# Third column group of the first ffn layer by seven products, with one buffer for turned weights and queries loaded by halves

## The chip, the cores and the metric

The kernel runs on one core of a Trainium2 chip. The metric is the device time of one launch in microseconds (us). All arithmetic is in fp32. TensorE is called PE below, its weight loads PEld, VectorE DVE, ScalarE ACT, GpSimd POOL, SyncE SP; "SPq" is SP's queue, which issues almost all DMAs.

## The reference, cut to what matters

```python
scores = scale * np.matmul(q, k.transpose(0, 1, 3, 2))        # q, k, v: (8, 8, 576, 64)
thresh = np.max(scores, axis=-1, keepdims=True) - tau
scores = np.where(scores >= thresh, scores, -1000000000.0)
attn = np.exp(scores - np.max(scores, axis=-1, keepdims=True))
attn = attn / (np.sum(attn, axis=-1, keepdims=True) + 1e-09)
x = np.matmul(attn, v)      # then (B,H,S,D) -> (4608 tokens, 512)
...
a = x @ w_a                 # w_a, w_b: (512, 1536)
b = x @ w_b
return (a * b @ w_out)      # w_out: (1536, 512)
```

The weights arrive as float64 and are turned into fp32 on the chip.

## The kernel before, in words

**Attention.** A pair is two heads of one batch; there are 32 pairs. A unit (i, u) is a tile of 128 queries of pair i (u = 0 to 3), or its last 64 queries (u = 4). The main loop (lines 760 to 842) has one step g for each unit, and an order written out by hand: `scores` (line 314: PE fills two PSUM tiles, DVE reduces the maximum), `turn_back`, `exchange_blocks`, `turn_blocks` of the unit before (DVE transposes in 32x32 blocks, then SP writes them to a `swap` tile in DRAM, lines 437 and 449), a portion of the ffn, `weigh` (ACT exp, DVE threshold and sum), `prep` of a coming pair, a second portion of the ffn, `weighted` of the unit four steps back (PE: product with v, line 475), `normalise`, loads, stores, two more portions of the ffn. `turn_back` (line 454) reads a finished `swap` tile back into a tile `wT`, the turned weights that `weighted` needs; `wT` has WT_BUFS = 2 buffers. The tile framework gives a buffer to a new tile when the old one's last reader is done. Every engine's queue keeps the order of the program.

**Queries and keys.** `load` (line 134) brings q and k of one pair by four DMAs each on SP's queue (576 x 64 per head, in pieces of 32 floats), q four steps and k three steps ahead; `prep` (line 294) turns a whole tile in place by one DVE transpose (line 297). `qT` and `kT` have HP = 4 buffers each. For the first four pairs PE does the turning (`prep_pe`, `turn_pe`, `diagonals`).

**Blocks for the ffn.** 256 tokens make a block; there are 18: two halves of each of 8 batches, and two blocks of the batches' last 64 tokens ("tail"). A block's x is a tile of 128 partitions x 4 x 256, written head pair by head pair. When it is complete, `exchange_blocks` (line 487) has POOL write a copy `xS` whose two halves of 64 partitions are swapped (eight copies, line 485), and the block joins the list `blocks`. `xT`, `xS`, the tail tile and early raw weights share six buffers (XT_BUFS).

**The ffn of a block** (`ffn`, line 549) is a generator that yields after each small group of matmuls; `advance` runs it for as many moving columns as the step's pace allows. PE is used as four tiles of 64x64: four matmuls, two row halves times two column halves, run side by side; I call them a quad. First layer: w_a and w_b have three column groups of 512 columns; a step f covers 256 of them, so f = 0..5, and f = 4, 5 are the third group. For each f and each matrix there are 8 quads of 256 columns (line 574) into one PSUM tile `pab`; ACT copies w_a's result to `h` (line 580), DVE multiplies w_b's result in (line 582). PSUM has four such tiles ("banks", two banks each), shared by scores (two), `pab`, `pv`, `po`. Second layer (line 617): already by seven products over 2x2 halves instead of eight, from the second block on (`state["sums"]`; the first block takes the long form, line 661), with sums of `h` made by POOL (`h_sums`, line 594) and sums of the outputs (line 586) by POOL, or by DVE once the attention is over (`state["over"]`). `h` has six buffers of 2 x 256.

**Pace.** A step may run 0.09 of a block's columns, in four portions (0.3, 0.35, 0.15, 0.2), but not more than what spreads the backlog to the next block's arrival, plus a part for a backlog of over one block. Blocks left over run after the last unit, with nothing else on the chip.

Of the kernel before, what the change touches and what calls it, by code (L numbers as in the profile page):

```python
# [24 lines left out]
XT_BUFS = 6  # L25
WT_BUFS = 2
H_BUFS = 6
OSB_BUFS = 5
# [23 lines left out]
def kernel(  # L52
# [81 lines left out]
    def load(i, name, engine=nc.sync):  # L134

        b, hp = pairs[i]
        src = {"q": q, "k": k}[name]
        t = work.tile([P, NB, Q], FP32, tag=name + "T", bufs=HP, name=name + "T")
        for j in range(2):
            rows = src[b, 2 * hp + j].rearrange("(n e) d -> e n d", e=Q)  # L140
            for h in range(2):
                r = slice((2 * j + h) * Q, (2 * j + h + 1) * Q)
                engine.dma_start(t[r], rows[:, :, h * Q:(h + 1) * Q])  # L143
        loaded.setdefault(i, {})[name] = t
# [40 lines left out]
    state = {"loaded": 0, "added": 0, "converted": 0, "rows": 0, "sums": False, "through": 0, "over": False}  # L185
# [5 lines left out]
    sums_of = sums_sb.rearrange("p (f n w) -> p f n w", n=3, w=CH)  # L191

# [101 lines left out]
    def prep(i, name):  # L294

        mT = loaded[i][name].rearrange("p n e -> p (n e)")
        nc.vector.transpose(mT, mT)
        prepared.setdefault(i, {})[name] = mT

    def prep_pe(i, name):  # L300

        m = loaded[i][name]
        mT = work.tile([P, S], FP32, tag=name + "T", bufs=HP, name=name + "T")
        tp = banks(SH, "tp")
        for c in range(2):
            for n in range(NR // 2):
                nc.tensor.transpose(tp[:, c, n * R:(n + 1) * R], m[:, c * (NR // 2) + n], ident[0:R, 0:R])
        prepared.setdefault(i, {})[name] = mT
        return mT, tp
# [4 lines left out]
    def scores(i, u):  # L314
        qT, kT = prepared[i]["q"], prepared[i]["k"]
        n = 2 if u < NT else 1
        sc = [banks(SH, "sc") for _ in range(n)]
        each = [(c, t, j) for c in range(2) for t in range(n) for j in range(2)]
        if units.index((i, u)) < BY_HEAD:
            each.sort(key=lambda x: x[2])  # L320
        for c, t, j in each:
            r = slice(j * D, (j + 1) * D)
            o = t if u < NT else 1 - j
            q0, to = (u * P + t * D if u < NT else MAIN), slice(o * D, (o + 1) * D)
            nc.tensor.matmul(sc[j if u < NT else 0][to, c], qT[r, q0:q0 + D],  # L325
                             kT[r, c * SH:(c + 1) * SH], start=True, stop=True)
        mx = small.tile([P, 2], FP32, tag="mx", name="mx")
        thr = small.tile([P, 2], FP32, tag="thr", name="thr")
        bias = small.tile([P, 2], FP32, tag="bias", name="bias")
        for j in range(n):  # L330
            c = slice(j, j + 1)
            nc.vector.tensor_reduce(mx[:, c], sc[j], axis=AX.XY, op=ALU.max)  # L332
        nc.vector.tensor_scalar(thr[:, 0:n], mx[:, 0:n], cut, None, op0=ALU.subtract)
        scored[i, u] = (sc, thr, bias, mx)
# [49 lines left out]
    def diagonals(i, u):  # L384

        ws, rcp = weights[i, u]
        dg = work.tile([P, 2, P], FP32, tag="h", bufs=H_BUFS, name="dg")
        for j in range(2):
            nc.scalar.activation(dg[:, j], ident, AF.Copy, scale=rcp[:, j:j + 1])
        weights[i, u] = (ws, dg)  # L390

    def turn_pe(i, u):
# [3 lines left out]
        wT = work.tile([P, NSLOT, P], FP32, tag="wT", bufs=WT_BUFS, name="wT")  # L396
# [57 lines left out]
    def turn_back():  # L454

        while ready:
            i, h = ready.pop(0)
            n = width(i, h)
            wT = work.tile([P, NSLOT, n], FP32, tag="wT", bufs=WT_BUFS, name="wT")
# [26 lines left out]

    def exchange_blocks():
        while complete:
# [4 lines left out]
            blocks.append(((x, xs), what))  # L493
# [54 lines left out]

    def ffn(xT, what):
# [3 lines left out]
        x, xs = xT  # L553
        hs = []
        n = CH // P
# [3 lines left out]
        for f, c0, c1 in steps:  # L559
            while (state["converted"] < 2 * HP * (f // n + 1)  # L560
# [3 lines left out]
            if c0 == 0:  # L564
                hs.append(work.tile([P, 2, HALF], FP32, tag="h", bufs=H_BUFS, name="h"))
            ht = hs[f][:, :, c0:c1]
            for w in (wa_sb, wb_sb):
# [15 lines left out]
                yield c1 - c0, 0, 0  # L583
        if state["sums"]:
# [21 lines left out]
            for both in ((1, 4), (2, 5), (7, 6), (3,)):  # L606
                po = banks(len(both) * CH, "po").rearrange("p r (m w) -> p r m w", w=CH)
                left = whole = len(both) * NF // 2 * CH
                for y, m in enumerate(both):
                    k, u, other = seven[m]  # L610
                    for f in range(NF // 2):
# [12 lines left out]
                        if m == 2 and f == NF // 2 - 1:  # L624
                            h_sums((1, 0), (1, 0), (0, 0), ALU.subtract)
                        if left:
# [62 lines left out]
    def cost():  # L689

        return BLOCK_COLS - (NF // 2 * CH if state["sums"] else 0)
# [3 lines left out]
    def advance(cols):  # L695
        running["owed"] += cols
        while running["owed"] > 0:
            if running["ffn"] is None:
                if not blocks:
                    running["owed"] = 0.0  # L700
                    return
                running["ffn"] = ffn(*blocks.pop(0))
# [23 lines left out]
    def backlog():  # L726
        return len(blocks) * cost() + (running["left"] if running["ffn"] is not None else 0)
# [14 lines left out]
    first = {i: g for g, (i, u) in enumerate(units) if u == 0}  # L742

# [16 lines left out]
    for g in range(len(units) + PV_LAG):  # L760
# [7 lines left out]
        turn_back()  # L768
# [27 lines left out]
        for p in range(HP, NPR):  # L796
            for name, d in (("q", 2), ("k", 1)):
                if g == first[p] - d:
                    prep(p, name)
        if g > BY_PE:  # L800
            advance(PORTIONS[1] * pace)
            n = g - PV_LAG
            if BY_PE <= n < len(units) and part(*units[n]):
                make_room()
                weighted(*part(*units[n]))
                running["owed"] -= (NSLOT + 1) // 2 * width(*part(*units[n]))
        for n in early.get(g, [])[:1]:
# [15 lines left out]
        for p in range(HP, NPR):  # L823
            for name, d in (("q", 4), ("k", 3)):
                if g == first[p] - d:
# [18 lines left out]
    exchange_blocks()  # L844
    state["over"] = True
    while blocks or running["ffn"] is not None:
# [35 lines left out]
```

## Time and profile before

| | |
|---|---|
| times of six runs | 1472.71, 1468.56, 1470.64, 1469.78, 1469.73, 1474.5 us; median 1470.21 us |
| the profiled execution | 1472.71 us, of which 1470.9 us are the span that the profile covers, 1.8 us lie around it |
| TensorE clock granted over the span | 0.995 |
| busy: PEld, DVE, ACT, POOL | 1213.2, 941.6, 677.5, 334.3 us |
| DMA | 220.75 MB, 150 GB/s on the mean; queue q1 (SP) has 216.52 MB of it |

The profile's page sums busy time by engine, cuts the span into 40 slices of 36.8 us, follows back the chain of work that ended last, and groups instructions by line and shape. An fp32 matmul stands in the trace as two matmul records and two weight loads. Records of one quad overlap, so a record's mean length is longer than its share of the time; rates are read from the distance between starts, or from busy time in a window.

### The profile page before, as it was taken

What the parts mean: (1) busy time and instruction counts of PE and PEld (TensorE: products, weight loads), DVE (VectorE), ACT (ScalarE), POOL (GpSimd) and SP (SyncE); (2) the same over time, 40 slices, a digit from 0 to 9 for tenths busy, and PEclk for the clock granted to TensorE, in tenths of its full rate; (3) what the DMA queues carried; (4) which work ended last, traced back from release to release, by engine and by line L of the source; (5) the groups of instructions that cost most, each with busy time, mean ns of one, the idle gap of its engine ahead of it and who ended that gap; (6) DMA issues with size and microseconds to landing.
All of it is one profiled execution on the core that took longest, in us unless ns stands there. A gap on an engine that the chain in (4) does not pass through costs nothing.

```text
span 1470.9 us, 57132 instructions
## 1 busy us (share of the span) xinstructions
PE 1418.8 (96%) x25344; PEld 1213.2 (82%) x25344; DVE 941.6 (64%) x2097; ACT 677.5 (46%) x1243; POOL 334.3 (23%) x504
## 2 busy tenths in 40 slices
PE   5779999999999999999999999999999999999998
PEld 4667677888879898897888998889888888888886
DVE  6998677677666776776656765577656766613212
ACT  5886455555554554554434544354544544411010
POOL 2773503122030403031312212120404040410000
PEclk9999999999999999999999999999999999999999
DMA  9967898798858976795647876588757976530000
GB/s 192 223 187 181 178 177 192 175 178 181 199 142 167 183 192 148 159 189 145 147 97 150 182 168 149 117 191 182 162 126 145 197 178 151 132 90 16 2 17 16
DMA packets 624582, 220.75 MB, mean 150 GB/s; under 512 B 542928, under 2 KB 612048, under 8 KB 624336
## 3 DMA queue, kind: packets, MB, share of 16 engines
q1 hardware_dynamic: 621968, 216.52, 67.4%
q8 instruction: 199, 3.26, 0.9%
q10 hardware_dynamic: 2368, 0.59, 0.2%
q14 instruction: 47, 0.39, 0.1%
HBM read 127.40 MB, written 89.65 MB: 148 GB/s over the span
## 4 chain that ended last, share of the span: by engine, by line
PE 86%; DVE 6%; DMA 4%; ACT 2%; SPq 2%; issue 1%; DVEq 0%; ACTq 0%
PE pab L574 46%; PE po L617 19%; PE sc L325 10%; PE pv L475 9%; DMA swap<-tw 2%; PE po L661 1%; DVE mx L332 1%; DVE tw L363 1%; DVE tw L429 1%; SPq L437 1%; DMA kT<-in_k_dram 1%; SPq L143 1%; DMA sums_u<-in_moe_w_a_dram 1%; DMA sums_u<-in_moe_w_b_dram 1%; DVE low L238 1%
## 5 line engine op out<-in xcount | busy, mean ns | idle before, releaser
L332 DVE TENSOR_REDUCE mx<-sc 128x1 f32<-128x576 f32 x288 | 205.2, 749 | 115.1 <-PE sc L325 104.3
L574 PE MATMUL pab<-xS,wa_sb 64*64 64x256 f32 (+1 forms) x3584 | 271.2, 370 | 1.3 <-issue 1.3
L574 PE MATMUL pab<-xS,wb_sb 64*64 64x256 f32 (+1 forms) x3584 | 267.8, 370 | 0.0
L325 PE MATMUL sc<-kT,qT 64*64 64x288 f32 x2304 | 244.1, 410 | 21.0 <-DVE kT L312 9.1
L574 PE MATMUL pab<-xT,wa_sb 64*64 64x256 f32 (+1 forms) x3200 | 237.8, 369 | 6.7 <-DVE tw L363 3.2
L586 POOL TENSOR_TENSOR h<-h 128x256 f32<-128x256 f32 x168 | 117.4, 732 | 547.5 <-PE po L617 544.4
L617 PE MATMUL po<-wo_sb,h 64*64 64x256 f32 x3264 | 241.4, 376 | 0.0
L574 PE MATMUL pab<-xT,wb_sb 64*64 64x256 f32 (+1 forms) x3200 | 236.2, 368 | 4.1 <-DVE h L582 2.7
L382 ACT ACTIVATE tw<-tw,rcp 128x576 f32<-128x576 f32 x244 | 176.1, 768 | 132.7 <-DVE rcp L376 132.6
L360 ACT ACTIVATE tw<-sc,bias,scalars 128x576 f32<-128x576 f32 x260 | 216.0, 831 | 19.3 <-DMA swap<-tw 10.4
L363 DVE SCALAR_TENSOR_TENSOR tw<-sc,thr,tw 128x576 f32<-128x576 f32 x260 | 203.7, 802 | 22.6 <-ACT tw L360 21.9
L574 PEld LDWEIGHTS pab<-xS,wa_sb 64*64 64x64 f32 x3584 | 194.5, 133 | 28.7 <-POOL xS L485 2.1
L574 PEld LDWEIGHTS pab<-xS,wb_sb 64*64 64x64 f32 x3584 | 195.3, 133 | 22.7 <-issue 0.2
L617 PEld LDWEIGHTS po<-wo_sb,h 64*64 64x64 f32 x3264 | 178.9, 132 | 22.9
L574 PEld LDWEIGHTS pab<-xT,wa_sb 64*64 64x64 f32 x3200 | 172.0, 133 | 30.4 <-DVE kept L465 4.3
L574 PEld LDWEIGHTS pab<-xT,wb_sb 64*64 64x64 f32 x3200 | 171.5, 133 | 24.7 <-DVE h L582 2.9
L325 PEld LDWEIGHTS sc<-kT,qT 64*64 64x64 f32 x2304 | 146.0, 134 | 52.6 <-issue 16.1
L475 PE MATMUL pv<-wT,vm 64*64 64x320 f32 (+3 forms) x2592 | 186.7, 377 | 1.7 <-DVE h L582 1.7
L617 PE MATMUL po<-sums_u,h 64*64 64x256 f32 x2448 | 181.3, 376 | 0.0
L429 DVE STREAM_TRANSPOSE tw<-tw 128x576 f32<-128x576 f32 x240 | 171.6, 753 | 0.0
L582 DVE TENSOR_TENSOR h<-h,pab 128x512 f32<-128x512 f32 (+1 forms) x112 | 73.4, 656 | 145.6 <-PE pab L574 139.5
L475 PEld LDWEIGHTS pv<-wT,vm 64*64 64x64 f32 x2592 | 143.7, 133 | 20.5 <-DVE h L582 2.6
(83 smaller groups left out, 1242.4 us busy)
## 6 DMA issues: line engine op xcount, KB each, us to landing
swap<-tw SPq DMA_DIRECT2D x240, 288.0 KB, 5.3
wT<-swap SPq DMA_DIRECT2D x28, 1440.0 KB, 7.5
wT<-swap SPq DMA_DIRECT2D x32, 1152.0 KB, 6.3
vm<-in_v_dram SPq DMA_DIRECT2D x32, 288.0 KB, 4.9
qT<-in_q_dram SPq DMA_DIRECT2D x112, 72.0 KB, 3.5
kT<-in_k_dram SPq DMA_DIRECT2D x112, 72.0 KB, 5.1
swap<-wt SPq DMA_DIRECT2D x112, 72.0 KB, 2.7
out_dram<-kept SPq DMA_DIRECT2D x30, 256.0 KB, 4.3
```

Source lines behind the costliest of these rows:

```text
L143: engine.dma_start(t[r], rows[:, :, h * Q:(h + 1) * Q])
L325: nc.tensor.matmul(sc[j if u < NT else 0][to, c], qT[r, q0:q0 + D], kT[r, c * SH:(c + 1) * SH], start=True, stop=True)
L332: nc.vector.tensor_reduce(mx[:, c], sc[j], axis=AX.XY, op=ALU.max)
L360: nc.scalar.activation(wb[j], sb[j], AF.Exp, bias=bias[:, j:j + 1], scale=e_scale)
L363: nc.vector.scalar_tensor_tensor(out=wv, in0=sb[j], scalar=thr[:, j:j + 1], in1=wv, op0=ALU.is_ge, op1=ALU.mult, accum_out=sums[:, j:j + 1])
L382: nc.scalar.activation(w, w, AF.Copy, scale=rcp[:, j:j + 1])
L429: nc.vector.transpose(w, w)
L475: nc.tensor.matmul(pv[j * D:(j + 1) * D, r], vm[rows, k0], wT[rows, k0], start=(s == (NT if j == r else 0)), stop=(s == NT - 1))
L574: nc.tensor.matmul(pab[c * D:(c + 1) * D, r], w[rows, f // n, k, fs + c * D:fs + (c + 1) * D], moving, start=(k == 0), stop=(k == H - 1))
L582: nc.vector.tensor_tensor(ht, ht, pab, op=ALU.mult)
L586: (nc.vector if state["over"] else nc.gpsimd).tensor_tensor(*a, **kw)
L617: nc.tensor.matmul(po[c * D:(c + 1) * D, r, y], ht[rows, t0:t0 + D], other[rows, f], start=(f == 0), stop=(f == NF // 2 - 1))
```

## The change

The third column group of the first layer is computed by seven products over 2x2 halves instead of eight. The three halvings are: the two matrices w_a and w_b; the 512 input features (two times 256); the block's 256 tokens (two times 128). Products have 128 moving columns. They need sums of weights, made once (`first_sums`), and sums of x, made by POOL for each block (`x_sums`, four operations on x and four on xS), and sums of products (ACT, DVE and POOL in `seven_of`). Storage is laid out anew: `wT` becomes one constant area (`turned_sb`), and `turn_back` is moved behind `weighted` in the step; q is loaded in two halves (256 and 320 queries) with three smaller buffers; `qT` and `dg` of the first four pairs live in the area that the weight sums take later; `h` has three buffers of twice the size. A block waits in `complete` until the block before it has left its first layer; only then are `xS` and the sums made.

```diff
-XT_BUFS = 6
-WT_BUFS = 2
-H_BUFS = 6
+XT_BUFS = 7
+H_BUFS = 3
+Q_BUFS = 3
...
     def load(i, name, engine=nc.sync):
...
+        n0, n1 = {"k": (0, NB), "q0": (0, HALF // Q), "q1": (HALF // Q, NB)}[name]
+        bufs = HP if name == "k" else Q_BUFS
...
-                engine.dma_start(t[r], rows[:, :, h * Q:(h + 1) * Q])
+                engine.dma_start(t[r], rows[:, n0:n1, h * Q:(h + 1) * Q])
...
-    def turn_back():
-
-        while ready:
+    def turn_back(count):
+
+        for _ in range(count):
             i, h = ready.pop(0)
             n = width(i, h)
-            wT = work.tile([P, NSLOT, n], FP32, tag="wT", bufs=WT_BUFS, name="wT")
+            wT = turned_at((i - 1) % HP * NSLOT * TAIL if n < HALF and i else NSLOT * HALF if n < HALF else 0, n)
             nc.sync.dma_start(wT, swaps.pop((i, h)).rearrange("(s r) p w -> (r p) s w", r=G))
...
+    def x_sums(x):
+
+        t = x_tile("xU").rearrange("p m (k n) -> p m k n", k=2)
+        b11, b12, b21, b22 = (x[:, k * 2:k * 2 + 2, n * P:(n + 1) * P] for k in range(2) for n in range(2))
+        for m, a, b in ((0, b12, b11), (1, b22, t[:, 0]), (2, b22, b12), (3, t[:, 1], b21)):
+            nc.gpsimd.tensor_tensor(t[:, m], a, b, op=ALU.subtract)
+        return t
+
     def exchange_blocks():
-        while complete:
+        while complete and not state["layer"] and not blocks:
             x, what = complete.pop(0)
             xs = x_tile("xS")
             for hp in range(HP):
                 exchange(x, xs, hp, 0, HALF, nc.gpsimd)
-            blocks.append(((x, xs), what))
+            blocks.append(((x, xs) + ((x_sums(x), x_sums(xs)) if state["first"] >= 3 else ()), what))
...
+    def first_sums(n):
...
+        nc.gpsimd.tensor_tensor(out, a, b, op=op)
+        state["first"] = n + 1
+
+    def seven_of(x, hg):
...
+        for m in (1, 6, 7, 5, 2, 4, 3):
+            w, moving = products[m]
+            pab = banks(2 * P, "pab")
+            left = 2 * HP * P
+            for y in range(2):
+                for k in range(HP):
+                    for r in range(2):
+                        rows = slice(r * D, (r + 1) * D)
+                        for c in range(2):
+                            w0 = y * P + c * D
+                            nc.tensor.matmul(pab[c * D:(c + 1) * D, r, y * P:(y + 1) * P], w[k][rows, w0:w0 + D],
+                                             moving[k][rows], start=(k == 0), stop=(k == HP - 1))
+                    left -= P
+                    if left:
+                        yield P, left, 2 * HP * P
+            got = pab.rearrange("p r (f n) -> p r f n", f=2)
+            if m in (1, 7, 5):
+                nc.scalar.copy(keep({1: "t1", 7: "t7", 5: "t5"}[m]), pab)
+            if m == 6:
+                nc.vector.tensor_tensor(keep("u2"), kept["t1"], pab, op=ALU.add)
+            elif m == 7:
+                pool(kept["t7"], kept["u2"], kept["t7"], op=ALU.add)
+            elif m == 5:
+                pool(kept["u2"], kept["u2"], kept["t5"], op=ALU.add)
+                pool(kept["t5"], kept["t7"], kept["t5"], op=ALU.add)
+            elif m == 2:
+                nc.vector.tensor_tensor(kept["t1"], kept["t1"], pab, op=ALU.add)
+            elif m == 4:
+                nc.vector.tensor_tensor(kept["t7"], kept["t7"], pab, op=ALU.subtract)
+                nc.vector.tensor_tensor(h0, *(kept[z].rearrange("p r (f n) -> p r f n", f=2) for z in ("t1", "t7")),
+                                        op=ALU.mult)
+            elif m == 3:
+                nc.vector.tensor_tensor(kept["u2"], kept["u2"], pab, op=ALU.add)
+                nc.vector.tensor_tensor(h1, *(kept[z].rearrange("p r (f n) -> p r f n", f=2) for z in ("u2", "t5")),
+                                        op=ALU.mult)
+            yield P, 0, 0
...
+            if f == (NG - 1) * n and len(xT) == 4:
+                groups.append(work.tile([P, n, 2, HALF], FP32, tag="h", bufs=H_BUFS, name="h"))
+                hs += [groups[-1][:, y] for y in range(n)]
+                yield from seven_of(xT, groups[-1])
+                break
...
                         if m == 2 and f == NF // 2 - 1:
                             h_sums((1, 0), (1, 0), (0, 0), ALU.subtract)
+                            state["layer"] = False
+                            exchange_blocks()
...
-        return BLOCK_COLS - (NF // 2 * CH if state["sums"] else 0)
+        return BLOCK_COLS - (NF // 2 * CH if state["sums"] else 0) - (2 * HP * P if state["first"] >= 3 else 0)
...
+                if len(blocks[0][0]) == 4 and state["first"] == 3:
+                    first_sums(3)
...
-        turn_back()
+        back = len(ready)
         exchange_blocks()
...
-            for name, d in (("q", 2), ("k", 1)):
-                if g == first[p] - d:
+            for name, d in (("q0", 2), ("k", 1), ("q1", 1)):
+                if g == (second if name == "q1" else first)[p] - d:
                     prep(p, name)
...
                 weighted(*part(*units[n]))
                 running["owed"] -= (NSLOT + 1) // 2 * width(*part(*units[n]))
+            turn_back(back)
...
-            for name, d in (("q", 4), ("k", 3)):
-                if g == first[p] - d:
+            for name, d in (("q0", 4), ("k", 3), ("q1", 3)):
+                if g == (second if name == "q1" else first)[p] - d:
                     load(p, name)
...
+        if g > first[HP] + 1 and not converting and state["first"] < 3:
+            first_sums(state["first"])
```

Here `second[p]` is the step of pair p's unit u = 2, and `state["layer"]` is set when a block's first layer begins.

## The prediction

> **What bounds the kernel now.** I read the page's busy times and slices first, then the busy time by stretches, then the chain that ended last.
>
> ```profile
> PE 1418.8 (96%) x25344; PEld 1213.2 (82%) x25344; DVE 941.6 (64%) x2097; ACT 677.5 (46%) x1243; POOL 334.3 (23%) x504
> ...
> PE   5779999999999999999999999999999999999998
> PEld 4667677888879898897888998889888888888886
> DVE  6998677677666776776656765577656766613212
> ```
>
> PE is full from the fourth slice to the last; no other engine comes near. The busy time by stretches (time, PE, PEld, DVE, ACT, POOL, granted clock, DMA share, GB/s) shows where it is not quite full:
>
> ```profile
> 240.00:400.00 160.00, 156.85 (x2704) 136.74 (x2700) 116.75 (x265) 84.08 (x152) 33.59 (x58) 0.99 0.85 187
> 400.00:520.00 120.00, 118.11 (x2077) 102.37 (x2073) 85.46 (x193) 60.50 (x111) 31.64 (x50) 1.00 0.80 170
> 520.00:720.00 200.00, 198.75 (x3563) 175.03 (x3559) 131.08 (x297) 94.97 (x170) 35.57 (x60) 1.00 0.73 160
> 1310.00:1380.00 70.00, 70.00 (x1297) 57.95 (x1289) 14.94 (x32) 6.82 (x13) 3.96 (x10) 1.00 0.03 10
> ```
>
> From 520 us on PE idles under 1% of the time, up to 520 us some 2%. Attention ends near 1320 us; then PE works through nearly three leftover blocks alone. The chain from 1300 us on, in order of time, gives the price of one layer:
>
> ```profile
> 1327.80 17.49 PE po L617 x325
> 1345.93 40.80 PE pab L574 x757
> 1387.37 17.49 PE po L617 x325
> 1405.50 40.80 PE pab L574 x757
> ```
>
> A first layer runs from 1345.93 to 1387.37, 41.44 us for 6 column steps x 2 matrices, so 41.44 / 12 = 3.453 us for one result of 8 quads x 256 = 2048 columns: 1.686 ns a column. What PE no longer has to do comes off the end almost whole, wherever it lay, as long as PE stays full.
>
> **The matmuls.** A third column group is 2 steps x 2 matrices = 4 results: 4 x 3.453 = 13.81 us. It becomes 7 products of 2 x 4 quads of 128 columns. Does a quad of 128 cost half of one of 256, with a weight load for half the columns? The first block ran in this shape. In the busy time of line 574 alone (time, PE, PEld):
>
> ```profile
> 54.61:55.48 0.87, 0.87 (x41) 0.87 (x36) 1.00 1.04 228
> ```
>
> This is one result half: 4 quads of 128, 512 columns, in 0.87 us (1.70 ns a column). Others of these runs that nothing interrupts take 0.87 too. So a product is 2 x 0.873 = 1.746 us and seven are 12.22 us: 13.81 - 12.22 = **1.59 us a block saved**. The weight loads just fit in: they were busy for all of that window, where they take 82% of PE's time in 256-column work. Bounds: 1.71 us (no loss by the narrower shape: 13.81 / 8) and, by the interrupted runs of 0.92 us, 13.81 - 7 x 1.84 = 0.93 us.
>
> [...] The window above has a load in every 27 ns, four tiles of the array loading side by side, and the measurement decides.
>
> How many blocks? The sums of weights wait for the conversion of the weights, which ends near step 15, and are made in steps 22 to 24. The block of steps 20 to 31 is exchanged before that, as is the first; the other **16 of 18** get the sums. 16 x 1.59 = **25.5 us less**.
>
> **Evacuation of PSUM (an added wait).** The group had 2 ACT copies and 2 DVE multiplications; it gets 3 copies (580 ns) and 6 DVE operations of 512 elements (674 ns, line 582): 0.6 us on ACT and 2.7 us on DVE a block, where PE spends some 75 us. As busy time that is covered: DVE has a third of its time free. But a PSUM tile now fills in 1.75 us instead of 3.45. During about half of a step the scores hold two of the four tiles; if then an evacuation ends more than 1.75 us after its product, PE stands still, and behind the waiting matmul are the next scores.
>
> ```profile
> ACT h L580 <- PE pab L574: 173.1, 61, 6.6
> DVE h L582 <- PE pab L574: 139.5, 41, 6.3
> ```
>
> ACT stood ready in 61 of 112 cases, DVE in only 41. I measured in the timeline, for each of the 112 pairs, from the end of the result's last matmul to the end of its evacuation. After 1310 us: 0.62 us ACT, 0.79 us DVE. From 520 to 1310 us the mean excess over 1.74 us is 0.15 us (ACT) and 0.25 us (DVE); from 300 to 520 us 0.40 and 0.71 us. With 3 ACT and 4 DVE evacuations: 3 x 0.15 + 4 x 0.25 = 1.45 us for a block in the middle (11 blocks), 3 x 0.40 + 4 x 0.71 = 4.04 us early (the two blocks between 262 and 410 us), nothing for the last three. All of it: 11 x 1.45 + 2 x 4.04 = 24 us. I take a quarter, since the scores hold their tiles for half the step and the pace lets only some two products through meanwhile: **+6 us**, with ends 0 and 24.
>
> [...]
>
> **POOL.** Per block 8 sums of 256 elements (732 ns, line 586) and 3 of 512 (about 1.3 us, between 732 ns and the 1.84 us of 768 elements): 9.8 us, 157 us in all; POOL goes from 23% to about a third. The row for swapped copies is 0.396 us x 8 = 3.2 us; they now start only when product 2 of the second layer is through, behind at most 12 x 0.73 us of `h` sums that began 2.6 us earlier: 9.4 us. PE has four more products to do, 4 x 2.59 = 10.4 us, and then 1.73 us that read only `xT`. Just covered; without cover up to 3 us a block. The x sums need 5.9 us and are used 28 us later. They delay output sums and so stores on SP by some us; nothing waits for those. DVE's durations beside a busy POOL are what they are without (the maximum: 747 and 748 ns), so more POOL work is no price on DVE. I take 0.
>
> **One buffer for turned weights.** `turn_back` now waits on SP for the products of the same step, behind it are loads for three steps ahead and one store.
>
> ```profile
> L460 SPq DMA_DIRECT2D wT<-swap x64: 376/382/1732, 110.7 to 1300.2; - x64
> ...
> DMA to landing us min/median/max: 3.5/6.7/8.9
> ```
>
> In the half with one result every two steps: two steps last 14.6 us early (the shortest neighbours 11.7), 16.4 later; less 2.2 us for the products and 0.4 for the issue, 12.0 us remain (shortest 9.1) for a landing of 6.7, at most 8.9. Covered, so 0. Were it short by a us, each of 28 such reads would cost PE that us, 28 us.
>
> **Queries by halves.** 28 x 4 more DMA issues on SP; an issue has a median of 0.6 us (line 143): 67 us over 1130 us, on a queue that also waits a lot. What suffers are key loads (DVE waits for them 6.1 us in all) and swap writes while DMA is at 85%, before 410 us. The other way, reads no longer stand at a step's head waiting for the swap to land (93.2 + 31.5 us of SP's waits). The chain has 1.7% swap landing, 0.8% and 0.6% SP issue, 0.7% key landing: 56 us is the most that could go or double. Nearest row 6.1 us: I take **+2 us**, ends -5 and +15. [...] `h` by double buffers costs 0: what frees a buffer precedes the next block's matmuls on PE.
>
> **Sum.** 1472.7 - 25.5 + 6 + 2 = 1455.2 us against the profiled execution (span 1470.9 + 1.8 around it). The median of the runs is 2.5 us below that execution: **1453 us**, -1.2%.
>
> **Rivals.**
> 1. *Evacuation becomes the bound (slower).* Place: third column group, PSUM tiles of lines 580 and 582 inside the attention. If DVE is everywhere as late as from 300 to 520 us (6 operations in a row instead of 2 push it there) and each excess counts: 13 x 4.04 = 52 us; -25.5 + 52 = +27: 1497 us. It decides from 25.5 / 13 = 2.0 us a block. For it: DVE late in 71 of 112 cases. Against: the median lateness of 0.82 us after 520 us, and waits of PE for DVE there of about 1 us in all.
> 2. *Little arrives.* If the steps of the attention are paced by their own DVE, ACT and DMA chain, only the last three blocks give: 3 x 1.59 = 4.8 us, 1465 us. For it: swap landings on the chain up to 365 us. Against: PE at 99% after 520 us.
> 3. *One buffer is late (slower).* +28 us by the above with the saving of 17.5: 1481 us. Against: 2 to 5 us of slack.
> 4. *Not what it says:* the sums ready later, say four blocks without: 1459 us.
> 5. *Clean.* No price at all: 1445 us; with -5 us from SP, 1440.
>
> **Numbers.** Forecast (1444 to 1461) 0.62; clean or better, below 1444, 0.04; rival 2 (1461 to 1473) 0.14; rival 4 0.04; rival 1 0.11; rival 3 0.05. The range of 1442 to 1470 leaves out rivals 1 and 3, a little of rival 2 and of the clean end. 0.2% is 2.9 us, about what a measurement can tell from no change: faster (below 1467.3) takes the forecast, clean, rival 4 and 0.10 of rival 2: 0.80; same 0.04; slower 0.16.
>
> **What would show it.** Matmuls of 64x128 in line `seven_of` at 0.87 us for 32 records; 224 x 2 x 16 = 7168 of them; the last two blocks' first layers 39.8 us instead of 41.4. Wrong if PE idles more than 10 us longer in the attention: before `pab` with DVE or ACT as releaser (rival 1), before `pv` with a DMA (rival 3), before scores with `kT` (queries); or if 32 narrow records take over 0.98 us, where the saving is gone.

## The result, and the profile after

The changed kernel takes 1476.7 us (median of 19 runs), the kernel before 1470.84 us beside it (43 runs): ratio **1.0041**, 95% interval 1.0032 to 1.0051. It is slower by 0.4% where 1.2% less was forecast. The profiled execution took 1479.74 us, its span is 1477.8 us, the granted clock over it 0.993. One of the twelve runs of a kernel below (side edits alone) was a slow one, 1496.39 us; without it that kernel's median is 1466.3 us instead of 1466.9.

A part of the difference goes with the clock. Its mean over the runs is 0.9943 in after and 0.9951 to 0.9960 in the four batches of before; among the runs of before, a clock lower by 0.001 goes with some 1.1 us more. That would be 1 to 2 of the 5.9 us. Whether the clock is a cause here or follows from the work, no run tells.

The page of the changed kernel, busy times and PE's slices:

```profile
PE 1409.1 (95%) x28416; PEld 1225.9 (83%) x28416; DVE 1000.3 (68%) x2195; ACT 685.9 (46%) x1259; POOL 489.2 (33%) x678
...
PE   5879999989999999999999999999999999999998
```

PE looks as full as before. It has 3072 matmul records more, which is 16 blocks x 192 (a block's third group had 4 x 64 = 256 records and has 7 x 64 = 448): the change reached the 16 blocks that were counted on. Its busy time fell by 1418.8 - 1409.1 = 9.7 us, not by 25.5, so the work that is left got 15.8 us longer. And PE now idles 1477.8 - 1409.1 = 68.7 us, before 1470.9 - 1418.8 = 52.1: 16.6 us more. Together 32.4 us are missing, and they are the 25.5 us of the forecast plus the 6.9 us by which the span grew.

The busy time by stretches of the changed kernel (columns as in the prediction):

```profile
240.00:400.00 160.00, 153.44 (x3004) 136.96 (x3000) 120.89 (x272) 83.61 (x151) 48.46 (x69) 0.98 0.83 182
400.00:520.00 120.00, 116.55 (x2304) 93.73 (x2298) 89.20 (x197) 58.22 (x107) 48.19 (x73) 1.00 0.74 155
520.00:720.00 200.00, 197.17 (x4150) 168.04 (x4146) 141.38 (x314) 98.08 (x177) 55.76 (x79) 1.00 0.75 168
1310.00:1380.00 70.00, 70.00 (x1505) 67.57 (x1501) 21.39 (x38) 8.01 (x16) 20.79 (x31) 1.00 0.14 38
```

Each stretch of the attention has more idle time of PE than before (6.6 us against 3.2, 3.5 against 1.9, 2.8 against 1.3); the stretch after it has none. The chain after 1340 us shows the same from its other side:

```profile
1356.00 27.36 PE pab L683 x507
...
1383.58 11.95 PE pab L622 x437
...
1395.63 18.13 PE po L728 x333
...
1413.98 27.36 PE pab L683 x506
```

Here all is as forecast. From one first layer to the next are 57.98 us, before 59.57: 1.59 us less, predicted 1.59. Seven products run from 1383.58 to 1395.63, 12.05 us, predicted 12.22. So the loss lies in the attention: the last unit's scores begin at 1284.0 us in the trace of before and at 1299.2 in that of after, 15.2 us later, though PE has less to do until then; after that mark the changed kernel is 8.3 us shorter.

What PE waits for between 240 and 1310 us in the changed kernel (engine, tile and line, what ended the wait: us in all, times, longest; before, no row is over 2.1 us in all):

```profile
PE pab L622 <- issue: 12.2, 11, 2.2
PE po L728 <- DVE t L640: 5.1, 4, 1.6
PE sc L337 <- issue: 4.1, 2, 3.4
PE pab L622 <- DVE u L631: 1.9, 2, 1.6
PE pab L622 <- DVE tw L375: 1.9, 2, 1.0
```

Line 622 is the matmul of the seven products, line 728 that of the second layer. Rows 2, 4 and 5 are waits for DVE; rows 4 and 5 stand where rival 1 put them, before `pab`, row 2 stands before the second layer's tile `po`. The largest row isn't for DVE: "issue" means that PE waited for nothing that the profile shows, no buffer and no semaphore, eleven times, each in the middle of a product. The timeline of one case (start, us, engine, line, operation, [idle before <- releaser]):

```profile
1181.49 1.52 PE L622 MATMUL pab<-xU,wb_sb 64*64 64x128 f32 x42
...
1185.23 0.77 PE L622 MATMUL pab<-xU,wb_sb 64*64 64x128 f32 x19 [2.21 <-issue]
```

After 42 of a product's 64 records PE stands still for over 2 us, with the tile, the weights and the x that it already uses.

**Theories.** (a) *Instructions* ("fetch theory" below): PE's instructions come by DMA, and come too late. The page lists their queue (packets, MB, share of 16 engines), before and after:

```profile
q8 instruction: 199, 3.26, 0.9%
```

```profile
q8 instruction: 223, 3.65, 1.0%
```

That is 16.4 KB a packet; PE began 57247 instructions (records, loads, semaphores) in after, 256 for each packet. A narrow product is 128 of them in 1.746 us, 73 a us; 256-column work is half that, 37 a us. So narrow work eats a packet in 3.5 us instead of 7. (b) *Evacuation* (reading results out of PSUM): seven results are read in place of four, and DVE, ACT and POOL are late (rival 1). (c) *The side edits* (queries by halves, one `wT`, order of the loads) cost something.

### The profile page after: what moved, and what is told of

It reads as the page before. It is cut to its first block, busy times and chain, and to the rows that moved or that the text cites. A ratio compares the mean times of both kernels' runs of the same rounds, so it can differ in the third digit from the quotient of the medians.

```text
span 1477.8 us, 63772 instructions
## 1 busy us (share of the span) xinstructions
PE 1409.1 (95%) x28416; PEld 1225.9 (83%) x28416; DVE 1000.3 (68%) x2195; ACT 685.9 (46%) x1259; POOL 489.2 (33%) x678
## 4 chain that ended last, share of the span: by engine, by line
PE 84%; DVE 7%; ACT 3%; issue 3%; DMA 2%; SPq 1%; ACTq 0%; DVEq 0%
PE pab L683 33%; PE po L728 20%; PE pab L622 11%; PE pv L491 10%; PE sc L337 9%; DVE mx L344 2%; PE po L774 1%; DVE tw L445 1%; DVE tw L375 1%; DMA swap<-tw 1%; SPq L154 1%; ACT tw L372 1%; DMA sums_u<-in_moe_w_b_dram 0%; DMA sums_u<-in_k_dram 0%; DVE xT L481 0%
## 5 line engine op out<-in xcount | busy, mean ns | idle before, releaser
L375 DVE SCALAR_TENSOR_TENSOR tw<-sc,thr,tw 128x576 f32<-128x576 f32 x260 | 202.5, 802 | 15.2 <-ACT tw L372 14.5
L588 POOL TENSOR_TENSOR t<-u,t 128x512 f32<-128x512 f32 x14 | 17.8, 1273 | 533.2 <-ACT t L629 533.2
L683 PE MATMUL pab<-xS,wa_sb 64*64 64x256 f32 (+1 forms) x2560 | 186.5, 368 | 0.4 <-issue 0.4
L683 PE MATMUL pab<-xS,wb_sb 64*64 64x256 f32 (+1 forms) x2560 | 182.9, 367 | 0.0
L491 PE MATMUL pv<-turned_sb,vm 64*64 64x320 f32 (+3 forms) x2592 | 179.0, 378 | 2.8 <-DVE h L691 1.7
L683 PE MATMUL pab<-xT,wb_sb 64*64 64x256 f32 (+1 forms) x2304 | 164.4, 367 | 4.5 <-DVE h L691 2.7
L683 PE MATMUL pab<-xT,wa_sb 64*64 64x256 f32 (+1 forms) x2304 | 158.5, 366 | 4.6 <-DVE tw L375 3.2
L491 PEld LDWEIGHTS pv<-turned_sb,vm 64*64 64x64 f32 x2592 | 133.0, 132 | 28.3 <-issue 3.5
L683 PEld LDWEIGHTS pab<-xS,wa_sb 64*64 64x64 f32 x2560 | 139.2, 134 | 15.5 <-POOL xS L501 2.1
L683 PEld LDWEIGHTS pab<-xS,wb_sb 64*64 64x64 f32 x2560 | 137.9, 133 | 13.3 <-issue 0.3
L728 PEld LDWEIGHTS po<-sums_u,h 64*64 64x64 f32 x2448 | 125.9, 134 | 20.6
L683 PEld LDWEIGHTS pab<-xT,wb_sb 64*64 64x64 f32 x2304 | 121.6, 134 | 18.8 <-DVE h L691 2.9
```

The costliest lines, as they stand in the source:

```text
L375: nc.vector.scalar_tensor_tensor(out=wv, in0=sb[j], scalar=thr[:, j:j + 1], in1=wv, op0=ALU.is_ge, op1=ALU.mult, accum_out=sums[:, j:j + 1])
L491: nc.tensor.matmul(pv[j * D:(j + 1) * D, r], vm[rows, k0], wT[rows, k0], start=(s == (NT if j == r else 0)), stop=(s == NT - 1))
L588: (nc.vector if state["over"] else nc.gpsimd).tensor_tensor(*a, **kw)
L683: nc.tensor.matmul(pab[c * D:(c + 1) * D, r], w[rows, f // n, k, fs + c * D:fs + (c + 1) * D], moving, start=(k == 0), stop=(k == H - 1))
L728: nc.tensor.matmul(po[c * D:(c + 1) * D, r, y], ht[rows, t0:t0 + D], other[rows, f], start=(f == 0), stop=(f == NF // 2 - 1))
```

## The experiments

### The parts alone

**Side edits alone.** The changed kernel without the sums of weights, so without products:

```diff
-        if g > first[HP] + 1 and not converting and state["first"] < 3:
-            first_sums(state["first"])
```

> The changed kernel without the seven products: the sums of the weights are never made, so all blocks take the long form of the third column group; one buffer for turned weights, its later read, queries by halves, double h buffers and the delayed exchange stay. Fetch theory (PE's instruction stream runs dry in the narrow products while the DMA engines are loaded) and evacuation theory (PE waits for PSUM tiles of the narrow products) both expect the time of the kernel before, 1467 to 1475 us. Side theory (the single buffer, the SP queue or the delayed exchange cost the 30 us that are missing) expects 1490 to 1505 us.

Measured: 1466.9 us, ratio 0.9971 (0.9959 to 0.9982). The side edits do not cost, they gain some 4 us. PE's idle time from 240 to 520 us falls from 5.0 us to 2.65:

```profile
240.00:520.00 280.00, 277.35 (x4854) 244.97 (x4850) 204.55 (x471) 146.43 (x264) 66.03 (x108) 1.00 0.84 180
```

Theory (c) falls, and the products are to be measured against 1466.9: with 25.5 us saved it would be 1441.4, and 35.3 us are to be found.

**Narrow matmuls alone.** The kernel before, whose third group runs in halves of 128 columns: the same four results, the same evacuations, only twice as many instructions for them.

```diff
-                for k in range(H):
+                for t0, k in [(z, k) for z in (range(0, c1 - c0, P) if f // n == NG - 1 else (0,)) for k in range(H)]:
+                    t1 = t0 + P if f // n == NG - 1 else c1 - c0
...
-                            nc.tensor.matmul(pab[c * D:(c + 1) * D, r],
+                            nc.tensor.matmul(pab[c * D:(c + 1) * D, r, t0:t1],
```

> The kernel before, its third column group computed as before, but each result in two halves of 128 columns: twice the instructions for it, the same columns, the same four evacuations at the same distance of 3.5 us. PE's own time grows by 16 x 0.873 - 13.81 = 0.16 us a block, 3 us in all. Fetch theory: 1 to 2 us more for each of some 15 blocks inside the attention, 1489 to 1504 us, with PE waits of the kind issue in the middle of the narrow runs. Evacuation theory: 1472 to 1476 us.

Measured: 1501.1 us, ratio 1.0202 (1.0172 to 1.0233). Its largest wait from 240 to 1310 us:

```profile
PE pab L575 <- issue: 12.8, 11, 2.2
```

Eleven waits for nothing, as in after, with no new evacuation at all. The narrower shape by itself costs 30 us, give or take some 5; 2 of them may go with the clock, whose mean is 0.9930 in these runs and 0.9951 in those of before beside them.

**Fewer evacuations.** Of the seven results three are not read, two are multiplied in directly:

```diff
-            if m in (1, 7, 5):
...
+            if m in (1, 7):
+                nc.scalar.copy(keep({1: "t1", 7: "t7"}[m]), pab)
+            if m in (4, 3):
+                nc.vector.tensor_tensor(h0 if m == 4 else h1,
...
```

> The changed kernel with its seven products, but products 6, 5 and 2 are never read, and 4 and 3 are multiplied in as they come: two ACT copies and two DVE multiplications as in the kernel before, none of the three POOL sums. The sums of products are left out, so the third group's h is not what it should be. Fetch theory: the waits at the start of a product (9 us) and of the second layer (8 us) go, those in the middle of a product stay: 1456 to 1463 us. Evacuation theory: nearly the whole saving appears, 1445 to 1450 us.

Measured: 1474.56 us, ratio 1.0016 (0.9998 to 1.0034), 2 us below after; both numbers missed.

```profile
PE pab L622 <- issue: 11.5, 12, 2.5
PE po L715 <- DVE h L631: 5.1, 4, 1.6
```

The two largest waits stand as they were: the second one is not made by the many sums, since here a single multiplication precedes the second layer. What it waits for shows in the timeline of after:

```profile
1107.59 0.65 DVE L640 TENSOR_TENSOR t<-t,pab 128x512 f32<-128x512 f32 x1
1108.27 0.69 DVE L641 TENSOR_TENSOR h<-t,t 128x512 f32<-128x512 f32 x1
1108.29 1.08 PE L728 MATMUL po<-wo_sb,h 64*64 64x256 f32 x14 [1.60 <-DVE t L640]
```

PE goes on 0.05 us after line 640 has read product 4 out of its PSUM tile, while line 641 is still making `h`. So the second layer waits for a PSUM tile and not for `h`; DVE came to line 640 late because maxima and transposes of the attention (2.8 us) stood ahead of it. At the other three stops of this row, too, PE goes on 0.05 us after line 640 has ended.

**Products spread out.** Each product follows one 256-column result, from the third on, so that narrow work comes in runs of half a packet:

```diff
+                if len(xT) == 4 and (f, w is wb_sb) > (0, True):
+                    if products is None:
+                        third = work.tile([P, n, 2, HALF], FP32, tag="h", bufs=H_BUFS, name="h")
+                        products = seven_of(xT, third)
+                    for step in products:
+                        yield step
+                        if not step[1]:
+                            break
```

> The changed kernel with another order: from the third 256-column result of the first layer on, each is followed by one of the seven products, so that narrow and wide runs alternate (a result of 3.45 us and a product of 1.75 us: some 49 PE instructions a us on the mean instead of 73). Fetch theory: most waits in the middle of products go, and products have 5.2 us to be evacuated: 1448 to 1457 us. Evacuation theory: 1450 to 1460 us, with no waits of the kind issue to be removed. Side theory: 1475 to 1479 us, no change.

Measured: 1468.55 us, ratio 0.9974 (0.996 to 0.9987), 8 us better than after, and well short of what was expected.

```profile
PE po L738 <- DVE t L640: 5.1, 4, 1.6
...
PE pab L622 <- issue: 1.6, 3, 1.0
```

The waits in products went from 12.2 to 1.6 us; the one before the second layer stayed.

### Is it DMA traffic?

**Less traffic.** The swap of the turned weights is left out from the ninth pair on (writes and reads; DMA share from 520 to 1310 us 0.13 instead of 0.72, 28 GB/s instead of 157), in after, and in the side edits alone:

```diff
-            for g in range(G):
+            for g in range(G if i < 2 * HP else 0):
...
-            nc.sync.dma_start(wT, swaps.pop((i, h)).rearrange("(s r) p w -> (r p) s w", r=G))
+            if i < 2 * HP:
+                nc.sync.dma_start(wT, swaps.pop((i, h)).rearrange("(s r) p w -> (r p) s w", r=G))
```

> The changed kernel, but from the third batch on the turned weights are neither written to DRAM nor read back: the products with v use what the second batch left, so the result is not the reference's from there on. All work of the engines stays; the greater part of the DMA traffic is gone for 11 of the 13 blocks that have seven products inside the attention. Fetch theory (instruction packets come late because the DMA engines are loaded): the waits of the kind issue and the small gaps in the narrow runs go, and the time falls by 18 to 28 us to 1449 to 1459 us. Rival (narrow runs are slow in the attention for a reason on the chip's engines: weight loads, PSUM, PE's own queue): it falls by as much as the kernel without the seven products falls when its swaps are left out, some 2 to 6 us, to 1470 to 1475 us.

> The same left out of the kernel that has all of the change but the seven products (1466.9 us with its swaps). Its PE has few waits to lose: both theories expect 1459 to 1466 us. The distance to the changed kernel without swaps is what the seven products bring without DMA traffic: fetch theory 12 to 20 us in favour of the seven products, the rival 5 to 12 us against them, as with swaps.

Measured: 1467.24 us with the products (0.9965, 0.9951 to 0.998) and 1467.74 us without (0.9966, 0.9951 to 0.998; 1459 to 1466 was expected). The traffic costs nothing without the products, and 1476.7 - 1467.24 = **9.5 us** with them. By the ratios, each against the kernel before in its own batch, it is 11.2 us, give or take 2.5. The waits of the kernel with products:

```profile
PE po L729 <- DVE t L641: 5.6, 4, 1.6
PE sc L337 <- issue: 4.1, 2, 3.4
...
PE pab L623 <- issue: 0.4, 1, 0.4
```

The waits for nothing in the products are gone. The row before the scores is the same with and without traffic, so it is another thing that the word "issue" covers. By the distances between starts, the time inside products beyond what their columns need falls from 21 to 5 us; the kernel gains less, since the waits at the starts of products grow from 8.9 to 10.4 us. It is a result between the theories: without traffic the products still bring 0.5 us instead of 25.5.

**Narrow, without traffic.** The narrow halves in the side edits, without swap:

> The kernel with all of the change but the seven products, with the third column group in halves of 128 columns, and from the third batch on without writing and reading back the turned weights (so not the reference's result from there on); evacuations as before. It tells how much of what narrow runs cost (30 us with DMA traffic: 1501.1 us) is the late instruction packets. Fetch theory: without traffic only the 3 us of PE's own time and the small gaps stay, 1470 to 1479 us. Rival (narrow runs are slow beside the attention in any case): 1488 to 1498 us.

Measured: 1476.75 us, ratio 1.0043 (1.0025 to 1.006), in the band of the first theory. Narrow halves cost 30.3 us with traffic (1501.1 - 1470.84) and 9.0 us without (1476.75 - 1467.74): **21 us** are the traffic's. By the ratios it is 30 - 11 = 18 us, and the two pairs stand on different kernels (before, and the side edits), so it is some 20 us. Of the 9.0 us, 2.8 are PE's own (18 blocks x 4 results x (2 x 1.746 - 3.453) us); the rest agrees with gaps of 60 to 150 ns within the narrow runs, some 6 us by the distances between starts.

**Traffic where there was none.** Loads of keys that nobody reads, in the tail until the last block:

```diff
+        if (complete or blocks) and rounds % 3 == 0:
...
+            t = work.tile([P, NB, Q], FP32, tag="kT", bufs=HP, name="kT")
...
+                    nc.sync.dma_start(t[r], rows[:, :, h * Q:(h + 1) * Q])
```

> The changed kernel with loads of keys that nothing reads, four DMAs for every third step of the tail until the last block begins. What counts is not the time but the narrow runs after the attention, where the changed kernel shows none of these waits: 11.95 us for the seven products of the block that ends near 1396 us. Fetch theory: waits of the kind issue appear there and the run takes 13 to 16 us, while the last block, without traffic, keeps 11.95 us. Rival: 11.95 us in both.

Measured: 1475.93 us, ratio 1.0029 (1.0011 to 1.0046). The chain in the last two blocks:

```profile
1379.20 8.34 PE pab L622 x301
1387.54 0.20 issue
...
1391.47 0.57 issue
...
1438.35 12.22 PE pab L622 x445
```

Seven products beside traffic (DMA share 0.56 from 1340 to 1400 us) take 13.4 us, with two waits for nothing that the tail had not had; the last block, almost without (0.22 from 1400 to 1460 us), takes 12.2, of which 0.2 lie ahead of the point from which the others are counted; in after both take 12.05. The stops can be made; at this traffic they are smaller than in the attention (0.57 us at most, against 2.2 in after).

**How the packets come late.** This was read from the traces: PE's instructions begun, counted against 256 for every packet. The highest count, reached whenever PE stands so, is taken for "none left". Instructions that PE still had, 240 to 1310 us and after:

| | when a packet starts: median, lowest | when it has landed: lowest tenth | landings with 4 or fewer left |
|---|---|---|---|
| before | 230, 128 | 136 | 0 of 149 |
| after | 216, 0 | 76 | 4 of 167 |
| after, without swap | 263, 120 | 148 | 0 of 169 |
| narrow alone | 211, 0 | 80 | 7 of 171 |
| narrow, without swap | 262, 105 | 129 | 1 of 175 |
| after, from 1310 us on | 270, 191 | 130 | 0 of 28 |

In the quiet part a packet starts with some 270 left; in none of these kernels does one start with more than 292. With its own 256 that makes 548, so by this count PE holds about two packets, an estimate. The packet itself takes 0.98 us (median from 240 to 1310 us) in before and in after. What traffic does is to delay its start: it starts with 216 left in after (median) and with 263 without the swap. And PE goes on only 1.2 to 1.9 us after the landing. All eleven waits of line 622 in after, and both of the tail with traffic, begin when PE has begun every instruction of the packets that it can use, and end that long after the next landing: the stop above ends at 1185.23, its packet started at 1181.78 and landed at 1183.28. By these numbers, as an estimate: 270 instructions last 7.3 us in 256-column work (37 a us) and 3.7 in narrow work (73 a us); about 2.5 us go for the packet (0.98) and what follows it (some 1.5), so narrow work bears some 1 us of delay, wide work near 5. What in the queues delays the start was not tried.

### Where the rest is

**Evacuations, without traffic.** The kernel with four evacuations, without swap:

> The changed kernel with four evacuations instead of seven (sums of products left out) and without the swaps from the third batch on. With swaps the missing evacuations brought 2 us. If the packets' lateness hid them: 1455 to 1462 us here. If evacuations do not matter: 1465 to 1468 us, as with all seven.

Measured: 1460.04 us, ratio 0.9917 (0.9896 to 0.9938). Three evacuations and the sums fewer now bring 1467.24 - 1460.04 = **7.2 us**, where with traffic they brought 2.1: the late packets had hidden them. The interval of the 7.2 is wide, some 3.7 us each way. The largest of its waits is still the one before the second layer:

```profile
PE po L716 <- DVE h L632: 5.4, 4, 1.6
```

In this kernel one operation empties the product's tile and makes `h`. That leaves 1460.04 - 1441.4 = 18.6 us. By the distances between starts in this kernel (250 to 1310 us), more than the columns need: 6.7 us at starts of products (a tile still held by scores, or DVE late), 8.0 before and in the second layer, 7.8 in small gaps within products; before had 1.3 us in its second layer. That is the size of what is left, but no run removed each part by itself.

**The products earlier.** As spread out above, but from the second result on, and all seven before the last 256-column result, so that the second layer follows on wide work:

```diff
-                if len(xT) == 4 and (f, w is wb_sb) > (0, True):
+                if len(xT) == 4 and (0, True) <= (f, w is wb_sb) < ((NG - 1) * n - 1, True):
```

> As the interleaved order (1468.6 us), but begun one result earlier, so that a 256-column result comes last: the second layer no longer waits for the sums of the last product (some 5 us of PE waits before po in the interleaved kernel). Expected 1462 to 1467 us; if these waits were hidden by something else, 1467 to 1470 us.

Measured: 1472.7 us, ratio 1.0004 (0.9989 to 1.0019): missed.

```profile
PE pab L681 <- DVE tw L375: 5.9, 7, 1.0
PE pab L681 <- DVE h L689: 3.9, 6, 1.4
```

The wait before the second layer is down to 0.6 us, and stands before the wide results instead.

**Two products in one tile.** Perhaps PE lacks tiles: two products take the halves of one PSUM tile, so that a product's evacuation has twice as long.

```diff
-            pab = banks(2 * P, "pab")
+            if m in (1, 7, 2, 3):
+                pair = banks(4 * P, "pab")
+            pab = pair[:, :, 0:2 * P] if m in (1, 7, 2, 3) else pair[:, :, 2 * P:4 * P]
```

> The changed kernel with two products in the two halves of one PSUM tile (1 and 6, 7 and 5, 2 and 4, then 3): four tiles for a column group as in the kernel before, filled in 3.5 us each, instead of seven. PSUM theory for the waits at the start of products (8.9 us in the profile) and before the second layer (6 us): they fall by 6 to 10 us, 1467 to 1472 us. Rival (these waits come from DVE's lateness, whatever the tiles): 1475 to 1479 us.

> Paired tiles, and from the third batch on without writing and reading back the turned weights (not the reference's result from there on). If late packets (9.5 us by the kernel without swaps) and PSUM tiles (6 to 10 us) are two losses that add: 1457 to 1462 us. If one hides the other, so that removing either shows the next: 1463 to 1468 us.

Measured: 1538.54 us (1.0473, 1.045 to 1.0496), and without swap 1539.86 (1.0467, 1.0447 to 1.0488). All expectations missed:

```profile
PE pab L624 <- ACT t L631: 30.0, 24, 4.8
PE pab L624 <- DVE t L640: 19.6, 12, 4.3
```

PE now waits before the second half until ACT or DVE has read the first, on semaphores that are part of the program; what the chip would do without them no run shows. The experiment said nothing on the number of tiles, but one thing: where PE stood anyway, traffic cost nothing (1538.54 us with it, 1539.86 without).

**Both halves read late.** The same, but the two products of a tile are read only when both are done:

```diff
+            both = {6: (1, 6), 5: (7, 5), 4: (2, 4), 3: (3,)}.get(m, ())
+            for e in both:
+                got = pair[:, :, 0:2 * P] if e in (1, 7, 2, 3) else pair[:, :, 2 * P:4 * P]
...
```

> Two products in the two halves of one PSUM tile, read only when both are done, so that PE never writes a tile that is being read: four tiles for a column group, as in the kernel before, each filled in 3.5 us. PSUM theory for the waits at the start of products (8.9 us) and before the second layer (6 us): 6 to 12 us less than the changed kernel, 1465 to 1471 us. Rival (DVE is late, whatever the tiles): 1474 to 1479 us.

> The same without writing and reading back the turned weights from the third batch on (not the reference's result from there on). If late packets (9.5 us) and PSUM tiles are two losses that add: 1455 to 1461 us. If one hides the other: 1463 to 1468 us, no better than the changed kernel without swaps (1467.2 us).

Measured: 1482.26 us (1.0073, 1.0049 to 1.0097), which misses both bands, and without swap 1467.55 (0.9972, 0.9958 to 0.9985), in the band of one loss hiding the other.

```profile
PE pab L624 <- issue: 11.2, 9, 3.1
PE po L732 <- DVE t L644: 6.9, 4, 2.3
```

By the distances between starts the waits at the starts of products fell from 8.9 to 0.8 us, so tiles were short there. But the sums now come later, and PE waits longer before and in the second layer (9.6 us became 14.3). The two make 3.4 us less, while the kernel takes 5.6 us more; its mean clock is 0.992, and the rest is not explained. My reading, not shown by a run: the lack of tiles isn't the cause by itself, DVE and ACT end late, and some wait of PE shows it.

### A version that beats both

**Products only where PE is alone.** The sums of weights are made so late that only the last three blocks have products:

```diff
-        if g > first[HP] + 1 and not converting and state["first"] < 3:
+        if g >= first[7 * HP] + 10 and not converting and state["first"] < 3:
```

> The changed kernel with the sums of weights made late (steps 150 to 152), so that only the last three blocks, which run after the attention or at its very end, have the seven products. If the products pay where PE is alone on the chip and only there: the kernel without them (1466.9 us) less 3 x 1.6 us, 1460 to 1464 us. If the loss in the attention has another cause than the products there (the order of blocks, POOL's exchange): no gain, 1466 to 1470 us.

Measured: **1463.01 us**, ratio 0.9945 (0.9929 to 0.9962), as expected: 3.9 us below the side edits alone (give or take some 3), for three blocks at 1.59 us (4.8).

## Why the prediction was wrong, step by step

- **What bounds the kernel.** "What PE no longer has to do comes off the end almost whole [...] as long as PE stays full": the condition failed. PE idles 16.6 us longer, and its work takes 15.8 us more than the forecast.
- **The matmuls: the step that failed first.** The price of 0.873 us for 32 records held where PE is alone (12.05 us for seven products, against the 12.22 worked out). It was carried to 13 blocks inside the attention, where it does not hold. It came from a stretch of three such runs, 192 instructions; that is fewer than the 270 that PE had left, as a median, at a packet's start after the attention, so it can't show what the 896 of seven products do. A longer narrow stretch of the first block, some 340 instructions from 95.05 us on, stood in the same trace, and it was stopped:

```profile
101.33 0.55 PE L574 MATMUL pab<-xS,wa_sb 64*64 64x128 f32 x11 [1.30 <-issue]
```

By the count of packets PE had none left here, and went on 1.5 us after a landing. In the attention the same shape loses some 20 us to late packets when it is alone (72 results), 9.5 us in the change. No rival had this. That the loads "just fit in" was no limit at all, as the last section shows.
- **Sixteen blocks.** Right, by the records.
- **Evacuation, +6 us out of 0 to 24: the step that failed second.** Right in kind, mis-sized. Three evacuations and the sums are 7.2 us by themselves, and waits at the starts of products (6.7 us) and before and in the second layer (8.0 us) stand for most of the 18.6 us that remain; if they are counted to this term, it is some 20 us, not 6. I had priced each evacuation's lateness against the next products' tiles, and took a quarter. I had not followed the end of the chain: the second layer takes the next PSUM tile 1.75 us after product 4, and DVE, with the attention's work ahead in its queue, has not emptied that product's tile (line 640). That wait is the largest of DVE's, 5.1 us in four stops.
- **POOL, 0.** Right: 33% busy as estimated, its sum of 512 elements took 1273 ns, estimated 1.3 us, and none of the waits of PE's matmuls is for POOL (its weight loads wait 5.7 us for `xS`, as much as before).
- **One buffer for turned weights, 0.** Right: PE never waits before `pv` for a DMA there.
- **Queries by halves, +2 us of -5 to +15.** The side edits as a whole gained 4 us, near the lower end; queries, buffers and order were not tried one by one.
- **The tail.** Right to 0.2 us.
- **The rivals.** "Evacuation becomes the bound" has the right sign and place; its 1497 us counted every excess, and it is only the smaller part of the loss that a run isolates. "Little arrives" (1465 us) is what the kernel would be with products in the last blocks alone (1463.01 us), but it reasoned from a pace by DVE and DMA, and these were not what stopped PE. My own test, "PE idles more than 10 us longer in the attention", came true, with "issue" as releaser, which I had not listed.

In sum, of 35.3 us (1476.7 against 1441.4), taken away in this order: **9.5 us** late instruction packets, shown by taking the traffic away; **7.2 us** the three added evacuations and the sums, shown without traffic (with it, 2.1); **18.6 us** lateness of DVE and ACT for PE's tiles and second layer and small gaps in narrow work, located in the trace, not taken apart. Open stays above all what makes the small gaps: they occur in the attention, not in the tail, with and without traffic.

## What to carry to other kernels

When an edit makes instructions smaller, count instructions per us beside bytes and columns: the stream of instructions had a queue of its own here (q8, 223 packets of 16.4 KB in after), and it ran out in narrow work. So a price measured on a short run of a shape need not hold for a long one: 0.87 us for 32 records held where PE was alone (12.05 us for seven products), and not in the attention, where late packets cost 9.5 us. Waits whose releaser is "issue", in the middle of work whose operands were in use already, were the sign (12.2 us in eleven waits); taking away the traffic beside them was the test (0.4 us were left). And an edit that saves time where one engine works alone can be put there alone: 1463.01 us, against 1466.9 without the products and 1476.7 with them in 16 blocks.

## What the runs showed of the hardware

- PE's instructions arrived in packets of 16.4 KB for 256 instructions (199 packets in before, 223 in after). From 240 us on a packet started with at most 292 left; from 240 to 1310 us it took 0.98 us (median in before and in after), and at the eleven stops of line 622 in after PE went on 1.2 to 1.9 us after a landing. At 73 instructions a us and a DMA share of 0.72 to 0.73 (520 to 1310 us) there were stops of up to 2.2 us in after, 3.1 in the kernel with both halves read late. In before line 574 had one such stop, 1.3 us at 101.33 us, and that in the first block's 128-column work; its 256-column work, at 37 a us, had none.
- A full PEld was no limit here. In 256-column work of the last block PEld is busy 26.00 of 26.00 us in after (1415 to 1441 us) and 33.69 of 41.00 in before (1346 to 1387 us), at the same pace of PE: 27.6 us for eight results in both (8 x 3.453; 1413.77 to 1441.34).
